# Two passes of 188 columns against two of 95, for the odd rows of every fourth wave number, in a fused Fourier mixing and ELU kernel

## The chip, the cores and the metric

The kernel runs on one core of one Trainium2 chip. The metric is the device time of one execution in microseconds (us), lower is better. Everything is computed in float32.

## The reference

```python
def _attn_ref(x):                       # x: (8, 3008, 256)
    X = np.fft.fft(x, axis=1)
    X = np.fft.fft(X, axis=2)
    return X.real.astype(np.float32)

def _moe_ref(x, w_in, w_out):           # x: the result above as (24064, 256)
    h = x @ w_in                        # w_in: (256, 2048)
    g = np.where(h > 0.0, h, 1.0 * (np.exp(np.minimum(h, 0.0)) - 1.0))
    return (g @ w_out).astype(np.float32)   # w_out: (2048, 256)
```

The real part of a two-dimensional Fourier transform is taken of each of the 8 batches (3008 rows, 256 channels), and every row of it goes through two matrix products with an ELU between them. The rows of the transform are mirror images of each other up to a sign, so the kernel computes only 1504 wave numbers k of each batch and gets the other half of the rows by a change of sign in the first product.

## The kernel before, in words

**The main loop.** The 8 times 1504 wave numbers stand as columns in two rings in SBUF, `Rr` (cosine part) and `Ir` (sine part). They are cut into 47 tiles of 256 columns. For each tile there are 8 steps, each with 256 of the 2048 hidden channels, so there are 376 steps. One step s does the following:

- TensorE: two matmuls `H<-Rr,Wsc` (`mm_P`) into a fresh PSUM bank H (there are three), later two `H<-Ir,Wsc` on top of them (`mm_Q`).
- VectorE: between these two, two instructions that read H (`even_part`, line 1339, written E), then `h_minus` (line 1353), and one step later the two ELU instructions `g_plus` and `g_minus` (line 1369), which finish the tile G of this step. The one that reads G and H is `g_plus`; with it H becomes free.
- ScalarE: four activations (two Relu, two Exp).
- GpSimd: four additions and subtractions `G<-G` of 256 columns (`sum_1`, `sum_3`, `sum_2`, `sum_4`, in that order; the second product is done by a scheme of seven products instead of eight).
- TensorE, two steps later: the seven products of the second layer into the banks pA to pD. The third of them, `pB<-G,WT`, reads the result of `sum_2`.

After every 8 steps a tile's sums are combined and transposed on VectorE (`u`, `v`, `ot`) and stored.

**The order.** Every piece of work is an event with a time on a made-up clock: step s begins at s*T, with T = 4.8, and an event stands at s*T + dt. All events are sorted by these times and issued in this order; `pin` keeps the order of each engine. So the times set only the order in each engine's queue, and an engine runs its queue strictly in this order. In step s, E stands at 0.9, `mm_Q` at 2.17, `g_plus` and `g_minus` of step s-1 at 2.2 and 2.9, `h_minus` at 3.55, and work besides goes to 4.2 or 4.25 (after `h_minus`, ahead of the next E) or to 1.0 (after E, ahead of `g_plus`).

**The transform of batches 2 to 7** (`Quarter`) is spread over the 48 steps of the main loop that come before its columns are needed. Steps of this part are counted from r0 = 48*b - 70 (for batch b = 2, r0 is 26). The 3008 rows have been folded to residues s = 0 to 752, on 94 to 96 partitions: four tiles `e`, `o` of 768 columns (near and far rows) for each part, ri = 0 (cosine) or 1 (sine), and for even or odd k (`kodd`). Each (ri, kodd) has two halves, each into one bank H: the even rows (`par` = 0) and the odd rows (`par` = 1). Each half is four passes, that is matmuls whose moving operand are columns of a constant table `QM` and whose stationary operand is one 128-column slot of the folded data. Each float32 matmul of the program is two records in the trace, each with its own weight load (PEld).

For even k the odd rows stand in two sets of 94 rows, s1 = 8p+3 or 8p+1 (slot 1 and its partner) and s3 = s1 + 376. `quarter_pairs` (GpSimd, at 46 to 49) makes sums u and differences v of each row with its mirror row, three slots in one instruction of 384 columns (line 601, `pairs<-e,o` and `o<-e,o`). The half then has these passes, with (u, v) exchanged for ri = 1:

```python
c = 378 if self.kodd else 379
for k, o in ((u, 0), (v, 189)) if self.kodd else ((u, 0),):
    yield (k, "+"), c, 95, slice(o, o + 189, 2)
    yield (k, "-"), c + 95, 94, slice(o + 1, o + 188, 2)
    c += 189
if not self.kodd:
    yield (v, 1), c, 188, slice(189, 377)
    yield (v, 3), c + 188, 188, slice(189, 377)
```

The first two passes (95 and 94 columns) give the 189 wave numbers k = 0, 4, 8 and so on; they use u1+u3 and u1-u3, which `shift_pairs` makes on VectorE. The last two (188 columns each) give the 188 wave numbers k = 2, 6, 10 and so on: one multiplies v1, the other v3, and both add into the same 188 columns.

For each of the two halves ri, `at_quarter` issues: even rows at step+0 (4.75), their reading on ScalarE (`copy`, 0.9) and VectorE (`unfold`, 1.0) at step+1, odd rows at step+2 (4.75), and at step+3 the `join` at 1.01: `plus` and `minus` add and subtract the even rows' result `es` (SBUF) and the odd rows' result (`odd`, in bank H) into the ring. With even k these are four VectorE instructions of 187 to 189 columns (`Rr<-bs,H`, `Ir<-bs,H`, line 598; more where the ring wraps), and for ri = 0 one more of one column. Step is r0+51 for ri = 0 and r0+56 for ri = 1, so the joins stand at r0+54 and r0+59. With odd k the same half already goes by passes of 95 and 94 columns in both parts, with `copy_odd` and `unfold_odd` (`spread`) ahead of its later join.

`turn` (line 870) is a VectorE instruction on 94x128: one slot times a scalar per row (from `twist_tab`), plus another slot.

Of the kernel before, what the change touches and what calls it, by code (L numbers as in the profile page):

```python
# [25 lines left out]
NE = 377  # L26
# [2 lines left out]
BE = 4 * NH  # L29
BW = BE + 3 * NE  # L30
NA = (95, 94)
QW = (944, 756)
NP = 47
SHIFT = 8 * NP
GW = 7 * TW
# [48 lines left out]
def _quarter_consts():  # L84

    p = np.arange(96)[:, None]

    def rows(m):
        s = 8 * p + m if m < 4 else 8 * (93 - p) + m
        return s, (p < (95 if m == 0 else 94)).astype(np.float64)  # L90

    low = _odd_rows()[:, None]
    valid = (p < 2 * NP).astype(np.float64)
    out = []
    for ri in range(2):
        fn = np.cos if ri == 0 else np.sin
        for kodd in range(2):

            def block(m, k):
                s, w = (low + SHIFT * (m == 3), valid) if m % 2 else rows(m)  # L100
                w = np.where(s == 0, 0.5, w)
                w = np.where(s == RUN, 0.5 if ri == kodd else 0.0, w)
                return w * fn(2.0 * np.pi * ((s * k[None, :]) % SEQ) / SEQ)

            def twist(m, n):
                s, w = (low, valid) if m % 2 else rows(m)
                a = np.arange(n)[None, :]
                phi = np.pi * s / HALF
                turn = 2.0 * np.pi * ((2 * a * s) % HALF) / HALF
                c, d = np.cos(phi), np.sin(phi)  # L110
                if ri:
                    return w * d * np.cos(turn), w * c * np.sin(turn)
                return w * c * np.cos(turn), -w * d * np.sin(turn)

            n = 94 if kodd else 95
            near = 2 * np.arange(n) + kodd
            a, b = block(0, near), block(4, near)
            if kodd:
                u1, v1 = twist(1, 189)
                u2, v2 = twist(2, 95)  # L120
                parts = [a, u2, b, v2, u1[:, ::2], -u1[:, 1::2], v1[:, ::2], -v1[:, 1::2]]
            else:
                ev, od = 4 * np.arange(189), 4 * np.arange(188) + 2
                parts = [a, b, block(2, ev[:95]), block(2, od[:94])]
                parts += [block(1, ev[::2]), block(1, ev[1::2]), block(1, od), block(3, od)]
            out += parts
    return np.concatenate(out, axis=1).astype(np.float32)


def _turn_consts():  # L130
    low = _odd_rows()
    out = []
    for s in (low, low + SHIFT, 8 * np.arange(96) + 2):
        t = np.tan(np.pi * np.minimum(s, RUN - 1) / HALF)
        out += [t, -1.0 / t, 1.0 / t, -t]
    for fn in (np.cos, np.sin):
        near, far = (fn(np.pi * s / HALF) for s in (low, low + SHIFT))
        out.append(far / near)
    return np.stack(out, axis=1).astype(np.float32)


# [34 lines left out]
def kernel(  # L176
# [386 lines left out]
            out=t[0:96, 0 : QW[kodd]], in_=QM_dr.ap()[:, n : n + QW[kodd]]  # L563
        )

    twist_tab = cpool.tile([128, 14], FP, tag="turns")

    warm = cpool.tile([128, 1], FP, tag="warm")
    nc.vector.memset(warm, 0.0)
# [30 lines left out]
    def gtt(o, a, b, op):  # L600
        pin(nc.gpsimd.tensor_tensor(out=o, in0=a, in1=b, op=op))  # L601
# [236 lines left out]
    def quarter_pairs(b, ri, kodd, m):  # L838

        near, far = state["F", ri, kodd]  # L840
        slot = lambda m: (near, far)[m // 4][0:94, 128 * (m % 4) : 128 * (m % 4) + 128]
        parts = state.setdefault(("Q", ri, kodd, b), {0: near[0:95, 0:128], 4: slot(4)})
        if not kodd:
            if m == 1:
                state["pairs"] = spool.tile(
                    [128, 384], FP, tag="side", bufs=2, name="pairs"
                )
            new = state["pairs"]
            a, z = (
                t[0:94, 128:512].rearrange("p (m d) -> p m d", d=128)  # L850
                for t in (near, far)
            )
            o = new[0:94].rearrange("p (m d) -> p m d", d=128)
            if m == 1:
                gtt(o, a, z[:, ::-1], ALU.add)
            else:
                gtt(z[:, ::-1], a, z[:, ::-1], ALU.subtract)
            for k in (1, 2, 3):
                parts["u", k] = new[0:94, 128 * k - 128 : 128 * k]
                parts["v", k] = slot(8 - k)  # L860
            return
        new = (near, near, far)[m - 1][0:94, (512, 640, 512)[m - 1] :]
        parts["u", m], parts["v", m] = new[:, 0:128], slot(1 if m == 1 else 8 - m)
        for i, o in ((0, parts["u", m]), (1, parts["v", m])):
            turn(o, slot(8 - m), 4 * (0, 2, 1)[m - 1] + 2 * ri + i, slot(m), ALU.add)

    def turn(o, a, c, b, op):

# [83 lines left out]
    class Dft:  # L952
# [27 lines left out]
        def unfold_odd(self):  # L980
            pass
# [39 lines left out]
    class Quarter(Dft):  # L1021
        def parts(self, par):

            u, v = ("v", "u") if self.ri and not self.kodd else ("u", "v")
            if not par:
                order = (
                    ((0, 94), (("u", 2), 95), (4, 94), (("v", 2), 95))
                    if self.kodd
                    else ((0, 95), (4, 95), ((u, 2), 95), ((v, 2), 94))
                )  # L1030
                c = o = 0
                for key, n in order:
                    yield key, c, n, slice(o, o + n)
                    c, o = c + n, o + n
                return
# [3 lines that stand above are left out]
                yield (k, "-"), c + 95, 94, slice(o + 1, o + 188, 2)  # L1039
                c += 189  # L1040
            if not self.kodd:
                yield (v, 1), c, 188, slice(189, 377)
                yield (v, 3), c + 188, 188, slice(189, 377)

        def mms(self, par, ps):
            parts = list(self.parts(par))
# [61 lines left out]

        def copy_odd(self):

            if self.kodd:
                self.far = spool.tile([128, NH], FP, tag="anti", bufs=2, name="far")
                act(self.far[0 : self.M, 0:189], self.odd[0 : self.M, 189:378])

        def unfold_odd(self):
            if self.kodd:
                t = spool.tile([128, NE], FP, tag="bs", bufs=BS, name="od")
                self.spread(t, self.odd, self.far, 188)
                self.odd = t

        def put(self, up, at, n, step, e, o):
            M = self.M
# [7 lines left out]
        def join(self, up):  # L1130

            M, kodd = self.M, self.kodd

            def run(t, start, step):
                return lambda i, z: t[0:M, steps_of(start + i * step, z - i, step)]

            base, top = kodd * RUN, kodd * RUN + RUN - 1
            if kodd:
                self.put(
                    up, base if up else top, NO, 1 if up else -1,  # L1140
                    run(self.es, 0, 1), run(self.odd, 0, 1),
                )
# [12 lines left out]
        def plus(self):  # L1155
# [822 lines left out]
    def at_quarter(step, b, ri, kodd, finish, join):  # L1978
        box = []

        def d():
            if not box:
                box.append(Quarter(ri, b, kodd, state["Q", ri, kodd, b]))
            return box[0]

        def half(par):
            d().ps = bank("H")
            d().mms(par, d().ps)

# [12 lines left out]

    for b in range(2, NB):
# [105 lines left out]
```

## Time and profile before

| | us |
|---|---|
| Median of 4 runs | 1910.21 (1909.8 to 1914.21) |
| The profiled execution, its time | 1909.85 |
| Its span on the core | 1908.1 |
| TensorE matmul busy | 1899.0 (100% of the span) |
| TensorE weight load busy | 1652.0 (87%) |
| VectorE busy | 1466.9 (77%) |
| GpSimd busy | 1349.6 (71%) |
| ScalarE busy | 877.1 (46%) |
| Mean granted TensorE clock | 1.0 of full speed |

The page of the profile gives each engine's busy time, the chain of work that ended last, and the costliest groups of instructions. A group's line reads: line of the kernel, engine, operation, output <- inputs, shapes, count, then busy us and mean ns of one, then the idle time of the engine just before them and what ended it. In a timeline each line has the start in us from the span's start, the time that the merged instructions cover, the engine, line, operation, tiles, shapes and count; in brackets is idle time before it and what ended that. A matmul's record is longer than the step to the next one, since matmuls are pipelined: what a matmul costs the engine is the distance of starts. VectorE's records also overlap by some 0.08 us when nothing waits.

### The profile page before, as it was taken

What the parts mean: (1) busy time and instruction counts of PE and PEld (TensorE: products, weight loads), DVE (VectorE), ACT (ScalarE), POOL (GpSimd) and SP (SyncE); (2) the same over time, 40 slices, a digit from 0 to 9 for tenths busy, and PEclk for the clock granted to TensorE, in tenths of its full rate; (3) what the DMA queues carried; (4) which work ended last, traced back from release to release, by engine and by line L of the source; (5) the groups of instructions that cost most, each with busy time, mean ns of one, the idle gap of its engine ahead of it and who ended that gap; (6) DMA issues with size and microseconds to landing.
All of it is one profiled execution on the core that took longest, in us unless ns stands there. A gap on an engine that the chain in (4) does not pass through costs nothing.

```text
span 1908.1 us, 27911 instructions
## 1 busy us (share of the span) xinstructions
PE 1899.0 (100%) x8972; PEld 1652.0 (87%) x8972; DVE 1466.9 (77%) x2788; ACT 877.1 (46%) x1711; POOL 1349.6 (71%) x1834
## 2 busy tenths in 40 slices
PE   9999999999999999999999999999999999999999
PEld 6888888888888888888888888888888888888887
DVE  8766667887878878778777787877878778777666
ACT  5754444444444444444444444444444444444443
POOL 4887657786677766777667777687766777556664
PEclk9999999999999999999999999999999999999999
DMA  9145211211011110111102111022110210100101
GB/s 339 45 33 43 57 24 46 52 24 36 12 44 41 32 33 12 46 41 30 31 19 49 34 28 30 13 56 44 24 24 16 55 21 15 17 12 15 20 12 23
DMA packets 278934, 73.80 MB, mean 39 GB/s; under 512 B 254402, under 2 KB 268998, under 8 KB 278788
## 3 DMA queue, kind: packets, MB, share of 16 engines
q1 hardware_dynamic: 270148, 61.58, 16.0%
q0 software_dynamic: 6464, 10.18, 1.7%
q8 instruction: 71, 1.16, 0.3%
q14 instruction: 75, 0.61, 0.1%
q10 hardware_dynamic: 2176, 0.26, 0.1%
HBM read 47.10 MB, written 24.80 MB: 38 GB/s over the span
## 4 chain that ended last, share of the span: by engine, by line
PE 96%; DVE 2%; DMA 1%; ACT 1%; issue 0%; POOL 0%; ACTq 0%; POOLq 0%; DVEq 0%
PE H L592 37%; PE pB L592 17%; PE pC L592 17%; PE pD L592 17%; PE pA L592 9%; DMA xl<-in_x_dram,ix 0%; DVE e L689 0%; DVE E L1339 0%; DVE o L689 0%; DVE pow L460 0%; POOL w L601 0%; ACT Wsc L604 0%; ACT G L604 0%; ACT M L604 0%; DMA wex<-wx 0%
## 5 line engine op out<-in xcount | busy, mean ns | idle before, releaser
L601 POOL TENSOR_TENSOR G<-G 128x256 f32<-128x256 f32 x1437 | 1045.9, 737 | 504.3 <-DVE G L1369 347.0
L604 ACT ACTIVATE G<-H 128x512 f32<-128x512 f32 x376 | 224.5, 597 | 929.7 <-DVE G L1353 926.0
L1339 DVE SCALAR_TENSOR_TENSOR E<-Rb,wex,H 128x256 f32<-128x256 f32 x752 | 327.8, 477 | 334.5 <-PE H L592 327.5
L592 PE MATMUL H<-Rr,Wsc 128*128 128x256 f32 x1504 | 387.9, 381 | 0.5 <-ACT Wsc L604 0.5
L592 PE MATMUL H<-Ir,Wsc 128*128 128x256 f32 x1504 | 386.9, 380 | 1.5 <-DVE E L1339 1.4
L592 PE MATMUL pC<-G,WT 128*128 128x256 f32 x1440 | 369.7, 379 | 0.0
L592 PEld LDWEIGHTS H<-Ir,Wsc 128*128 128x128 f32 x1504 | 278.6, 189 | 49.1 <-DVE E L1339 3.9
L592 PEld LDWEIGHTS H<-Rr,Wsc 128*128 128x128 f32 x1504 | 282.6, 190 | 41.1 <-issue 2.3
L592 PEld LDWEIGHTS pC<-G,WT 128*128 128x128 f32 x1440 | 274.1, 190 | 36.7
L1353 DVE SCALAR_TENSOR_TENSOR G<-E,H 128x512 f32<-128x512 f32 x376 | 257.4, 685 | 44.8 <-POOL G L601 11.4
L1369 DVE SCALAR_TENSOR_TENSOR G<-G,H 128x512 f32<-128x512 f32 x376 | 256.4, 682 | 39.6 <-ACT G L604 39.5
L1369 DVE SCALAR_TENSOR_TENSOR G<-M,G 128x512 f32<-128x512 f32 x376 | 257.4, 685 | 0.8 <-ACT M L604 0.8
L604 ACT ACTIVATE G<-G 128x512 f32<-128x512 f32 x376 | 233.4, 621 | 0.0
L592 PE MATMUL pA<-G,w 128*128 128x256 f32 x784 | 229.6, 380 | 0.0
L592 PE MATMUL pB<-G,w 128*128 128x256 f32 x784 | 229.6, 380 | 0.0
L592 PE MATMUL pD<-G,w 128*128 128x256 f32 x784 | 229.4, 379 | 0.0
L604 ACT ACTIVATE M<-G 128x512 f32<-128x512 f32 x376 | 224.2, 596 | 2.8 <-DVE G L1353 2.8
L604 ACT ACTIVATE M<-M 128x512 f32<-128x512 f32 x376 | 221.1, 588 | 0.1
L592 PE MATMUL pB<-G,WT 128*128 128x256 f32 x720 | 214.5, 380 | 0.0
L592 PE MATMUL pD<-G,WT 128*128 128x256 f32 x720 | 214.3, 379 | 0.0
L592 PEld LDWEIGHTS pA<-G,w 128*128 128x128 f32 x784 | 149.1, 190 | 20.5 <-DVE G L1369 0.3
L592 PEld LDWEIGHTS pB<-G,w 128*128 128x128 f32 x784 | 149.1, 190 | 20.2 <-PE H L592 0.2
(172 smaller groups left out, 1556.1 us busy)
## 6 DMA issues: line engine op xcount, KB each, us to landing
out_dram<-ot SPq DMA_DIRECT2D x496, 32.0 KB
xq<-in_x_dram SPq DMA_DIRECT2D x48, 94.0 KB
out_dram<-ot SPq DMA_DIRECT2D x256, 2.0 KB
Rb<-r SPq DMA_DIRECT2D x10, 376.0 KB
raw<-in_moe_w_in_dram SPq DMA_DIRECT2D x7, 512.0 KB
MC<-dft_mats SPq DMA_DIRECT2D x3, 943.5 KB
xq<-in_x_dram SPq DMA_DIRECT2D x12, 192.0 KB
xq<-in_x_dram SPq DMA_DIRECT2D x36, 64.0 KB
```

What stands on the lines that cost most here:

```text
L592: nc.tensor.matmul(out_, lhsT=lhsT, rhs=rhs, start=start, stop=stop, skip_group_check=True)
L601: pin(nc.gpsimd.tensor_tensor(out=o, in0=a, in1=b, op=op))
L604: pin(nc.scalar.activation(out=o, in_=i, func=func, **kw))
L1339: nc.vector.scalar_tensor_tensor(out=S.E[:, c], in0=Rb[:, cols(i)], scalar=wex[:, f : f + 1], in1=S.H[:, c], op0=ALU.mult, op1=ALU.add,)
L1353: nc.vector.scalar_tensor_tensor(out=two(S.G[:, 0:512])[:, :, ::-1], in0=two(S.E), scalar=2.0, in1=two(S.H), op0=ALU.mult, op1=ALU.subtract,)
L1369: nc.vector.scalar_tensor_tensor(out=o, in0=e, scalar=-1.0, in1=h, op0=ALU.add, op1=ALU.max)
```

## The change

For k = 4n+2 the angle of row s is (2n+1)*phi with phi = pi*s/752, and the row s3 = s1 + 376 turns it by an odd number of quarter circles. So the two rows' contributions can be drawn together ahead of the matmul: for each a = 0 to 94, two sums

- y-part: sum over the rows of cos(phi)*cos(4*a*phi) * y, with y = v1 - tan(phi)*v3
- z-part: sum over the rows of -sin(phi)*sin(4*a*phi) * z, with z = v1 + v3/tan(phi)

give n = 2a by their sum and n = 2a-1 by their difference (for ri = 1 with sine and cosine exchanged in the table). The change does so for even k in batches 2 to 7:

- the two passes of 188 columns become two of 95, into columns 189 to 283 and 284 to 378 of the bank H;
- y and z are made by two new `turn` instructions on VectorE for each ri (`turn_pairs`), y into free columns of the far tile, z in place of v3; they are issued at r0+51 (4.2) and r0+52 (4.25) for ri = 0, at r0+53 (4.2) and r0+57 (4.25) for ri = 1;
- in the join's step, ahead of it, a `copy_odd` on ScalarE (95 columns from H to `far`) and an `unfold_odd` on VectorE (two instructions of 94 columns, `spread`, into a new SBUF tile `od` of the pool `bs`);
- the second and fourth instruction of the join read `od` (SBUF) in place of H;
- `quarter_pairs` writes its sums for even k into free columns of the near and far tiles and not into a tile `pairs` of its own, so the one GpSimd instruction of 384 columns becomes one of 256 and one of 128;
- the constant table `QM` has 758 columns for even k, 944 before, and `twist_tab` 16 columns, 14 before.

```diff
-QW = (944, 756)
+QW = (758, 756)
...
-                parts += [block(1, ev[::2]), block(1, ev[1::2]), block(1, od), block(3, od)]
+                parts += [block(1, ev[::2]), block(1, ev[1::2]), *twist(1, 95, RUN)]
...
+    t = np.tan(np.pi * low / RUN)
+    out += [-t, 1.0 / t]
...
-            o = new[0:94].rearrange("p (m d) -> p m d", d=128)
+            z = z[:, ::-1]
+            homes = (near[0:94, 512:768], 0, 2), (far[0:94, 512:640], 2, 3)
             if m == 1:
-                gtt(o, a, z[:, ::-1], ALU.add)
+                for o, lo, hi in homes:
+                    o = o.rearrange("p (m d) -> p m d", d=128)
+                    gtt(o, a[:, lo:hi], z[:, lo:hi], ALU.add)
...
+    def turn_pairs(b, ri, k):
+
+        parts = state["Q", ri, 0, b]
+        f = "vu"[ri]
+        a, z = parts[f, 1], parts[f, 3]
+        o = z if k == "z" else state["F", ri, 0][1][0:94, 640:768]
+        turn(o, z, 14 + "yz".index(k), a, ALU.add)
+        parts[f, k] = o
...
             if not self.kodd:
-                yield (v, 1), c, 188, slice(189, 377)
-                yield (v, 3), c + 188, 188, slice(189, 377)
+                for n, k in enumerate("zy" if self.ri else "yz"):
+                    o = 95 * n
+                    yield (v, k), c + o, 95, slice(189 + o, 284 + o)
...
         def copy_odd(self):
 
-            if self.kodd:
-                self.far = spool.tile([128, NH], FP, tag="anti", bufs=2, name="far")
-                act(self.far[0 : self.M, 0:189], self.odd[0 : self.M, 189:378])
-
-        def unfold_odd(self):
-            if self.kodd:
-                t = spool.tile([128, NE], FP, tag="bs", bufs=BS, name="od")
+            c, n = (189, 189) if self.kodd else (284, 95)
+            self.far = spool.tile([128, NH], FP, tag="anti", bufs=2, name="far")
+            act(self.far[0 : self.M, 0:n], self.odd[0 : self.M, c : c + n])
+
+        def unfold_odd(self):
+            t = self.od = spool.tile([128, NE], FP, tag="bs", bufs=BS, name="od")
+            if self.kodd:
                 self.spread(t, self.odd, self.far, 188)
-                self.odd = t
+            else:
+                self.spread(t, self.odd[:, 189:284], self.far, 94)
...
-                    run(self.odd, 189 * h + first // 2, 1),
+                    run((self.odd, self.od)[h], first // 2, 1),
...
         if kodd:
             at(finish * T + 4.26, lambda: d().finish())
-            at((step + 3) * T + 0.9, lambda: d().copy_odd())
-            at((step + 3) * T + 1.0, lambda: d().unfold_odd())
+        at((step + 3) * T + 0.9, lambda: d().copy_odd())
+        at((step + 3) * T + 1.0, lambda: d().unfold_odd())
...
+        for step, dt, ri, k in (
+            (51, 4.2, 0, "y"), (52, 4.25, 0, "z"), (53, 4.2, 1, "y"), (57, 4.25, 1, "z"),
+
+        ):
+            rel(step, dt, turn_pairs, b, ri, k)
```

The order of the instructions on TensorE stays as it was, with as many of them.

More of the change, by code (lines that the diff above doesn't have):

```diff
@@ L103, in block, with twist @@
                 return w * fn(2.0 * np.pi * ((s * k[None, :]) % SEQ) / SEQ)
-            def twist(m, n):
+            def twist(m, n, span=HALF):
                 s, w = (low, valid) if m % 2 else rows(m)
                 a = np.arange(n)[None, :]
-                phi = np.pi * s / HALF
-                turn = 2.0 * np.pi * ((2 * a * s) % HALF) / HALF
+                phi = np.pi * s / span
+                turn = 2.0 * np.pi * ((2 * a * s) % span) / span
                 c, d = np.cos(phi), np.sin(phi)
@@ L564, in load_quarter_mats @@
         )
-    twist_tab = cpool.tile([128, 14], FP, tag="turns")
+    twist_tab = cpool.tile([128, 16], FP, tag="turns")
     warm = cpool.tile([128, 1], FP, tag="warm")
@@ L843, in quarter_pairs @@
         if not kodd:
[L844 to L848, printed above, removed]
             a, z = (
@@ L852, in quarter_pairs @@
             )
-            o = new[0:94].rearrange("p (m d) -> p m d", d=128)
+            z = z[:, ::-1]
+            homes = (near[0:94, 512:768], 0, 2), (far[0:94, 512:640], 2, 3)
             if m == 1:
-                gtt(o, a, z[:, ::-1], ALU.add)
-            else:
-                gtt(z[:, ::-1], a, z[:, ::-1], ALU.subtract)
+                for o, lo, hi in homes:
+                    o = o.rearrange("p (m d) -> p m d", d=128)
+                    gtt(o, a[:, lo:hi], z[:, lo:hi], ALU.add)
+            else:
+                gtt(z, a, z, ALU.subtract)
+            for o, lo, hi in homes:
+                for k in range(lo, hi):
+                    parts["u", k + 1] = o[:, 128 * (k - lo) :][:, 0:128]
             for k in (1, 2, 3):
-                parts["u", k] = new[0:94, 128 * k - 128 : 128 * k]
                 parts["v", k] = slot(8 - k)
@@ L1140, in join @@
                     up, base if up else top, NO, 1 if up else -1,
-                    run(self.es, 0, 1), run(self.odd, 0, 1),
+                    run(self.es, 0, 1), run(self.od, 0, 1),
                 )
```

## Prediction

> **What bounds the kernel now.** I read the page first: busy times, then the chain that ended last.
>
> ```profile
> PE 1899.0 (100%) x8972; PEld 1652.0 (87%) x8972; DVE 1466.9 (77%) x2788; ACT 877.1 (46%) x1711; POOL 1349.6 (71%) x1834
> ...
> PE 96%; DVE 2%; DMA 1%; ACT 1%; issue 0%; POOL 0%; ACTq 0%; POOLq 0%; DVEq 0%
> ```
>
> TensorE is busy all the time and 96% of the chain. A busy matmul engine can still wait, so the second view is the waits of TensorE over the whole run:
>
> ```profile
> PE H L592 <- DVE E L1339: 1.4, 3, 0.7
> PE H L592 <- ACT Wsc L604: 1.2, 2, 0.6
> ```
>
> These are the longest entries, and nearly all of it lies before 216 us. So in the part that the change touches (432 to 1650 us) the time is the sum of TensorE's steps: a step taken out shortens the run by its length, and whatever makes TensorE wait lengthens it by the wait. The third view is the timeline of TensorE at one odd half (batch 2, ri = 0), then at an even half, which has eight records of 94 and 95 columns:
>
> ```profile
> 442.59 0.58 PE L592 MATMUL H<-QM,e 94*128 94x95 f32 x4
> 443.01 0.83 PE L592 MATMUL H<-QM,o 94*128 94x188 f32 x4
> 443.68 1.03 PE L592 MATMUL H<-Rr,Wsc 128*128 128x256 f32 x4
> ```
>
> ```profile
> 457.06 0.36 PE L592 MATMUL H<-QM,e 95*128 95x95 f32 x2
> 457.26 0.61 PE L592 MATMUL H<-QM,o 94*128 94x95 f32 x4
> 457.70 0.39 PE L592 MATMUL H<-QM,pairs 94*128 94x94 f32 x2
> 457.93 0.84 PE L592 MATMUL H<-Rr,Wsc 128*128 128x256 f32 x3
> ```
>
> From start to next start, the odd half takes 443.68 - 442.59 = 1.085 us (to the ns) and the even half 457.93 - 457.06 = 0.865.
>
> **TensorE: what goes.** The odd half becomes eight records of 94 and 95 columns, like the even half, in the same order. The saving is 1.085 - 0.865 = 0.22 us a half. All twelve odd halves of even k (6 batches, 2 ri) measure 1.084 to 1.086, and every half of 95-column passes 0.863 to 0.866, so 12 x 0.2205 = **2.65 us**. Halving the columns doesn't halve the step: 188 columns step by 159 ns (the first of four by 190), 95 by 111 to 113, with a weight load of 190 ns per record beside each. A step as short as 84 to 86 ns stands in the trace too, once per half, in its first record.
>
> The Trainium skill, "TensorE: Matmul & The Clock Gate", section "Back-to-back issue gap", gives about 81 ns per matmul for a stream of weight loads and matmuls at 128 columns, less than the 111 ns that these rows show; by it the four records would come to 0.12 us less a half, 1.5 us in all, and the run to an estimated 1906.1. The rows are this kernel's own float32 passes of the same width, and I go by them.
>
> **VectorE: what is added.** In all 24 turns, 24 spreads of 94 columns, and 24 join instructions that read SBUF instead of H. The only question is what is queued behind them and when TensorE needs it. Here is VectorE's timeline around the first join:
>
> ```profile
> 438.91 0.87 DVE L1339 SCALAR_TENSOR_TENSOR E<-Rb,wex,H 128x256 f32<-128x256 f32 x2 [0.98 <-PE H L592]
> ...
> 441.12 0.69 DVE L1353 SCALAR_TENSOR_TENSOR G<-E,H 128x512 f32<-128x512 f32 x1
> 441.73 1.16 DVE L870 SCALAR_TENSOR_TENSOR o<-o,twist_tab,e 94x128 f32<-94x128 f32 x2
> 444.75 0.87 DVE L1339 SCALAR_TENSOR_TENSOR E<-Rb,wex,H 128x256 f32<-128x256 f32 x2 [1.85 <-PE H L592]
> 445.54 1.13 DVE L598 TENSOR_TENSOR Rr<-bs,H 128x189 f32<-128x189 f32 x4
> 446.57 0.15 DVE L598 TENSOR_TENSOR R<-bs,H 128x1 f32<-128x1 f32 x1
> 446.64 0.68 DVE L1369 SCALAR_TENSOR_TENSOR G<-G,H 128x512 f32<-128x512 f32 x1
> ```
>
> *The turns.* One takes 354 to 372 ns here when it begins with GpSimd free or just starting, 770 to 777 beside it (the pair at 441.73 is one of each). All four go ahead of an E that waits for TensorE anyway: the idle time before that E is 1.65 us at r0+52, 0.98 at r0+53, 1.85 at r0+54 and 1.21 at r0+58. Even at 0.78 each turn fits (the tightest is z, 0.78 in 0.98). I cost the four at nothing. If the cover were gone, each us past it would be a us on TensorE, since `H<-Ir` starts only 0.22 us after E's end.
>
> *The join, ri = 0.* The two spreads go between E and the join. Instructions of 94 and 95 columns step by 0.165 us (four of them fill 435.40 to 436.06 in the same timeline), so `g_plus` at 446.64 comes 2 x 0.165 = 0.33 us later against TensorE. Behind it wait `g_minus`, `h_minus` and, on other engines, these two:
>
> ```profile
> 443.51 0.72 POOL L601 TENSOR_TENSOR xq<-xq,xq 96x255 f32<-96x255 f32 x1
> 447.47 3.03 POOL L601 TENSOR_TENSOR G<-G 128x256 f32<-128x256 f32 x4 [3.23 <-DVE G L1369]
> ```
>
> ```profile
> 449.72 0.59 PE L592 MATMUL pB<-G,w 128*128 128x256 f32 x2
> 450.16 0.59 PE L592 MATMUL pB<-G,WT 128*128 128x256 f32 x2
> ```
>
> GpSimd's four sums of G start when `g_plus` is done; the third ends at 449.69 and feeds `pB<-G,WT` at 450.16, so 0.47 us lie between. Not all of that is free: where this product really waited (at 214.84), it started 0.09 after the sum's end and its next step was 0.07 longer, so 0.16 are needed and the **slack is 0.31 us**. It is 0.46 to 0.47 at four of the six joins; at 915.7 and 1151.2 (batches 4 and 5) the ring wraps, the join has two instructions more, and 0.335 - 0.16 = 0.18 is left. The stall is then 4 x (0.33 - 0.31) + 2 x (0.33 - 0.18) = **0.4 us**. Everything here moves with TensorE's 0.22 us, because E waits for TensorE in front of the join.
>
> *The SBUF operand.* For `Rr<-bs,od` of 188 columns this trace has no row; its bounds are near ones. From below: 128 columns from SBUF alone take 275 ns, as 124 from H do (277), so no difference. From above: `bs<-xq` of 188 columns, SBUF alone beside a busy GpSimd, reaches 882 to 885 against 346 from H, +0.54 each. I take nothing, since GpSimd is idle from 444.24 to 447.47 (3.23 us in the fence) and the join ends at 446.73.
>
> *The other slacks behind `h_minus`.* The E after it waits 0.98 us; ScalarE's chain has 0.38 us before `p<-pA` (449.93), which waits for TensorE. 0.33 fits in both.
>
> *The join, ri = 1.* The same 0.33 us, but an even half of TensorE lies behind, and the sum ends 1.43 us before its product (1.31 where the ring wraps): nothing.
>
> **ScalarE and GpSimd.** `copy_odd` (0.25 us, as `near<-H` of 95 columns) goes ahead of two Exp and waits for the odd half's end; the Exps end at 443.96 and `g_plus` comes at 446.64, so 2.7 us cover it; past that it would delay `g_plus` like the spreads. GpSimd's 384 columns (0.995 us) become 256 and 128 (0.73 and 0.48), 0.22 us more at r0+46 and r0+48, where it then idles 0.78 and 0.51 us: nothing; without that idle time the sums would be late, with 0.66 us or more to their product. The smaller table is six batches' constant, loaded once each: nothing.
>
> The Trainium skill, "GPSIMD Engine Reference", section "Key points", says that GpSimd shares its SBUF interfaces with VectorE and contends with instructions of two SBUF inputs, as all the added turns and SBUF joins are. The rows bear that out (354 against 777), and by the rule alone the join would pay the +0.54 twice, which is the second rival below.
>
> **Sum.** -2.65 + 0.4 = -2.25 us on the profiled execution's 1909.85 gives 1907.6. Three of the four runs and the profile lie at 1909.8 to 1910.21; the median shown is 0.36 above the profile, and I put half of that on top: **1907.8**.
>
> **The rivals.**
> - *The join's spreads cost more.* If the new dependences (spread on `far`, join on `od`) each lose the 0.08 us overlap of records, g_plus is 0.49 late: 4 x 0.18 + 2 x 0.31 = 1.3 us. Result 1909.85 - 2.65 + 1.3 + 0.2 = 1908.7. Against it: an instruction stands between the second spread and its reader.
> - *Slower: the SBUF joins meet GpSimd.* At the six joins of ri = 0, `g_plus` is then 0.33 + 2 x 0.54 = 1.41 us late, and `pB<-G,WT` stalls 4 x 1.10 + 2 x 1.23 = 6.9 us; 1909.85 - 2.65 + 6.9 + 0.2 = 1914.3. It decides from a lateness of about 0.7 us on (6 x 0.44 eats 2.65). For it: `Rr<-bs,od` of 376 columns takes up to 1073 ns at the joins of odd k. Against it: GpSimd's idle time around this join, in all six batches.
> - *The saving is hidden* (TensorE waits for something right after, in every half, or the short passes take what the long ones did): 1909.9 to 1910.2. Against it: no wait of TensorE over 0.2 us between 216 and 1890 us.
> - *Passes are shorter than the 111 ns*: at the 86 ns of the first records, 48 x 0.0255 = 1.2 us more; with no stall 1909.85 - 2.65 - 1.2 + 0.2 = 1906.2. Against it: from the second record on, none of the short passes goes below 109.
>
> **How the numbers follow.** About 0.2% (3.8 us) is what a measurement of this kernel can tell from no change. Chances: forecast (1907.2 to 1908.3) 0.66; costlier spreads 0.09; hidden 0.08; shorter passes 0.09 (faster by over 0.2%, below 1906.4); meeting GpSimd 0.08, of which 0.07 above 1914.0. So faster 0.09, same 0.84, slower 0.07. The range leaves out the last two cases: 1906.7 to 1910.0; the upper end takes in the hidden case, the lower a forecast without stall and shorter by 0.5 us.
>
> **What would show it.** Right: odd halves of 0.865 us; E at r0+54 still waiting for TensorE; `g_plus` 0.33 us later after E; gaps of `pB<-G,WT` under 0.2 us, in batches 4 and 5 above all. Wrong: an `Rr<-bs,od` far over 0.35 us, an E without idle time ahead of it at r0+52 to r0+58, a new wait of TensorE on VectorE or GpSimd in its list of waits.

## The result, and the profile after

The changed kernel takes **1907.34 us** (median of 32 runs, 1906.59 to 1911.62), the kernel before 1909.79 us (median of 52 runs, 1909.02 to 1919.6). The ratio is 0.9987 with a 95% interval of 0.9982 to 0.9992. So it is faster, by 2.45 us between the medians, and inside the 0.2% that the prediction counts as no change. The profiled execution took 1906.76 us, with a span of 1904.9 at a granted clock of 1.0.

First the page after: busy times, then the chain that ended last.

```profile
PE 1897.0 (100%) x8972; PEld 1649.5 (87%) x8972; DVE 1487.9 (78%) x2836; ACT 879.4 (46%) x1723; POOL 1350.8 (71%) x1846
...
PE 96%; DVE 2%; ACT 1%; DMA 0%; issue 0%; POOL 0%; ACTq 0%; SPq 0%; DVEq 0%; POOLq 0%
```

The balance is the same. TensorE has as many records as before (8972) and 2.0 us less busy time. VectorE has 48 instructions more (24 turns, 24 spreads) and 21 us more busy time, in a run that is shorter. That work was hidden, so what is left to explain is on TensorE.

Next, the timeline of TensorE at the first odd half after the change (start, length, engine, line, operation, operands, records).

```profile
441.34 0.58 PE L594 MATMUL H<-QM,e 94*128 94x95 f32 x4
441.76 0.61 PE L594 MATMUL H<-QM,o 94*128 94x95 f32 x4
442.21 1.06 PE L594 MATMUL H<-Rr,Wsc 128*128 128x256 f32 x4
443.10 0.59 PE L594 MATMUL pA<-G,w 128*128 128x256 f32 x2
```

From the first record of the half to the first of `H<-Rr` it is 0.87 us instead of 1.085, as forecast. But look one group further: `H<-Rr` takes 0.89 us to `pA` (442.21 to 443.10). Behind the long passes the same four records took 0.86. Record by record, in ns from start to start (the last four steps are those of `H<-Rr`):

```
before  86 110 111 111 | 190 160 159 159 | 220 215 215 215
after   86 110 110 112 | 113 111 112 112 | 245 216 217 215
```

Of the 220 ns that the short passes save, the first step behind them takes back 25.

To place the rest, I cut both runs at the first and last record of a scalar product (`QM`) on TensorE. The part ahead starts with the kernel, the section between holds everything that the change touches, and the part behind is output.

| | first `QM` record at | section | from the last `QM` record to the end |
|---|---|---|---|
| before | 432.20 us | 1256.45 us | 219.43 us |
| after | 430.95 us | 1254.53 us | 219.43 us |

The section is 1.92 us shorter. Step by step its records give:

- twelve odd halves, 0.2205 us shorter each: -2.65 us
- the step behind each of them, 0.0255 us longer: +0.31 us
- a stall of `pB<-G,WT` at the join in batches 4 and 5: 0.155 and 0.160, together +0.32 us
- the same place in the four other batches, 0.017 to 0.024 each: +0.08 us
- all else: +0.02 us

Of the 1.25 us by which the section starts earlier, 0.86 has built up by 17 us into the run and all by 114 us, long before anything that the change computes. What it is belongs to the last experiments.

### The profile page after: what moved, and what is told of

It is laid out like the page before. It is cut to its first block, busy times and chain, and to the rows that moved or that the text cites. A ratio compares the mean times of both kernels' runs of the same rounds, so it can differ in the third digit from the quotient of the medians.

```text
span 1904.9 us, 27983 instructions
## 1 busy us (share of the span) xinstructions
PE 1897.0 (100%) x8972; PEld 1649.5 (87%) x8972; DVE 1487.9 (78%) x2836; ACT 879.4 (46%) x1723; POOL 1350.8 (71%) x1846
## 4 chain that ended last, share of the span: by engine, by line
PE 96%; DVE 2%; ACT 1%; DMA 0%; issue 0%; POOL 0%; ACTq 0%; SPq 0%; DVEq 0%; POOLq 0%
PE H L594 37%; PE pB L594 17%; PE pC L594 17%; PE pD L594 17%; PE pA L594 9%; DVE e L691 0%; DVE o L691 0%; DVE pow L462 0%; DVE E L1352 0%; POOL w L603 0%; DMA xl<-in_x_dram 0%; ACT Wsc L606 0%; ACT G L606 0%; ACT M L606 0%; DVE w L420 0%
```

## The experiments

**Theories.** *A (the prediction's):* the time is the sum of TensorE's steps. The short passes take out 12 x 0.22 us, and the spreads return about 0.4, because they delay `g_plus`, GpSimd's sums of G and so `pB<-G,WT`. *B:* the missing part went elsewhere, into the short passes themselves or into some other effect of the added work. *C:* GpSimd and VectorE meet at the SBUF operands, so that the join costs far more. The first two experiments part A from B by making one half of the change alone.

### The added work alone

Edit of the kernel before: turns, copies and spreads are made, into columns and tiles that nothing reads; passes and join stay.

```diff
+        turn(state["F", ri, 0][1][0:94, 512 + n : 640 + n], z, 14 + "yz".index(k), a, ALU.add)
...
+            t = self.od = spool.tile([128, NE], FP, tag="bs", bufs=BS, name="od")
             if self.kodd:
...
+            else:
+                self.spread(t, self.odd[:, 189:284], self.far, 94)
```

> The kernel before with all that the change adds and nothing that it removes: the four turns of each batch (y and z into spare columns), copy_odd and the two spreads, but the passes of 188 columns stay and the join reads H as before; the new tile od is not used. Theory (everything added lies beside TensorE, but for the join of ri = 0 where the ring wraps): TensorE's odd halves stay at 1.085 us, the product that reads the third sum stalls 0.15 us in batches 4 and 5 and by under 0.03 in the others, so +0.3 to +0.4 us on the kernel before, ratio 1.0002. Rival (the added VectorE work costs something at each of the twelve halves): 12 x 0.165 us or more, so +2 us or more, ratio 1.001 and up, with TensorE's waits on VectorE in the list.

Measured: 1909.8 us against 1909.58 of the kernel before, ratio 0.9999 (0.9991 to 1.0008). In the trace the section is 1256.76 us, 0.31 longer than before. `g_plus` starts 2.22 us after E (2.35 where the ring wraps) instead of 1.89, and the stall is almost all at the two wraps. So 24 turns and 24 spreads (20 us of VectorE) and 12 more copies on ScalarE cost TensorE 0.3 us in six batches. B's second form (some other effect of the added work) is out.

### The short passes alone

Edit of the changed kernel: no turns and no spreads; the passes take rows 1 and 3 as they are, and the join reads H. It leaves out the combination of those rows, so wave numbers 2, 6, 10 and so on are not the reference's.

```diff
-                for n, k in enumerate("zy" if self.ri else "yz"):
+                for n, k in enumerate((1, 3)):
...
-                    run((self.odd, self.od)[h], first // 2, 1),
+                    run(self.odd, 189 * h + first // 2, 1),
...
-            rel(step, dt, turn_pairs, b, ri, k)
+            pass
```

> The changed kernel with the two short passes alone: no turns, no copy_odd, no spreads for even k, and the join reads H; what it leaves out is the combination of the rows 1 and 3, so the wave numbers 2, 6, 10 and so on of batches 2 to 7 are not the reference's. Theory: the odd halves take 0.865 us and nothing stalls at the joins, so -2.65 us on the kernel before (ratio 0.9986) and 0.3 us less than the changed kernel. Rival (the saving is larger on TensorE and partly lost to the added work): more than 3.2 us under the kernel before.

Measured: 1906.79 against 1909.58 us, ratio 0.9985 (0.9976 to 0.9994). In the trace the section is 1254.14 us, 2.30 shorter than before, without a stall. The passes alone are worth 2.30 us, not 2.65. The steps of its first odd half are 86, 110, 111, 111, 113, 111, 112, 112 and then 246, so the 26 ns behind each half belong to the short passes: 12 x 0.0255 = 0.31. B's first form holds for that part. The kernel before has them behind each of its even halves too; at the first one `H<-Rr` takes 0.89 us to `pA`:

```profile
433.07 1.06 PE L592 MATMUL H<-Rr,Wsc 128*128 128x256 f32 x4
433.96 0.60 PE L592 MATMUL pA<-G,w 128*128 128x256 f32 x2
```

In its odd halves about as much stands in the first long pass (190 ns against 159 or 160 of the others), inside the 1.085 us. So the two halves that the prediction compares were not cut at like places.

### The stall taken away

The wait of batches 4 and 5 is easy to miss. The list of TensorE's waits has no entry for it. It shows in TensorE's timeline of the changed kernel, as a step that is too long, and, below it, in the row of the weight loads:

```profile
918.12 0.60 PE L594 MATMUL pA<-G,w 128*128 128x256 f32 x2
918.55 0.60 PE L594 MATMUL pB<-G,w 128*128 128x256 f32 x2
919.03 0.70 PE L594 MATMUL pB<-G,WT 128*128 128x256 f32 x2
```

```profile
918.33 0.41 PEld L594 LDWEIGHTS pB<-G,w 128*128 128x128 f32 x2
919.03 0.30 PEld L594 LDWEIGHTS pB<-G,WT 128*128 128x128 f32 x2 [0.29 <-POOL G L603]
```

The first `pB` starts 0.43 after `pA`, the second 0.48 after the first, and its pair of records lasts 0.70 instead of 0.60: 0.05 and 0.10 are lost. The weight load names the releaser, GpSimd's sum of G. In this edit `g_minus` and `h_minus` stay in their place, and the half of the join that nothing needs so soon goes behind them:

```diff
-        at(t + 0.001, lambda: d().minus())
+        at(t + (0.001 if kodd or ri else 3.25), lambda: d().minus())
```

> The changed kernel with one event moved: for ri = 0 of even k the minus half of the join is issued at 4.25 of the same step (behind h_minus) and not at 1.0 (ahead of g_plus). Theory: g_plus comes 0.6 us earlier, the two stalls of 0.15 us in batches 4 and 5 are gone, the idle time before the next E is used up to the same degree, so -0.3 us on the changed kernel, seen in the trace rather than in the time. Rival (the idle time before the next E is needed for something else): a new wait of TensorE on E in the step after, 0.1 us or more at each of six joins, and the time is the changed kernel's or above.

Measured: 1906.99 against 1909.58 us, ratio 0.9988 (0.9979 to 0.9996). In the trace `g_plus` starts 1.64 us after E (1.77 in batch 4), the sum ends 0.58 to 0.73 us ahead of its product, and the section is 1254.14 us, 0.38 shorter than with the whole change. TensorE's timeline of this kernel at the same place:

```profile
918.30 0.59 PE L594 MATMUL pA<-G,w 128*128 128x256 f32 x2
918.73 0.59 PE L594 MATMUL pB<-G,w 128*128 128x256 f32 x2
919.16 0.59 PE L594 MATMUL pB<-G,WT 128*128 128x256 f32 x2
```

Every group starts 0.43 behind the one before it. So the stall is 0.4 us in all and comes from the join's length, as A has it. This version has the lowest median of those that compute everything; against the changed kernel the 0.35 us (0.14 when each is set against the kernel before that was measured beside it) are too little for a timed difference, and only the traces tell them apart.

### What a short pass costs

If the passes are limited by their columns, halving them again saves; if by the weight load that each record brings, it costs. The first edit cuts each pass of 95 into 48 and 47. The second, made when the first was measured, pads the table with zeros and makes the passes 128 columns wide, 33 of them of no use.

```diff
-                    o = 95 * n
-                    yield (v, k), c + o, 95, slice(189 + o, 284 + o)
+                    for o, m in ((95 * n, 48), (95 * n + 48, 47)):
+                        yield (v, k), c + o, m, slice(189 + o, 189 + o + m)
```

> The changed kernel with each of the two passes of 95 columns cut into one of 48 and one of 47 with the same stationary operand, so the same columns in twice as many records. Theory (a record cannot step faster than its weight load, 111 ns, however few its columns): four records more of 111 ns a half, and the shorter ones are no faster, so 12 x 0.446 = +5.3 us on the changed kernel. Rival (the step goes with the columns): +0 to +1 us, since the columns are the same in all.

```diff
-                    o = 95 * n
-                    yield (v, k), c + o, 95, slice(189 + o, 284 + o)
+                    o = 128 * n
+                    yield (v, k), c + o, 128, slice(189 + o, 317 + o)
```

> The changed kernel with 33 columns of zeros behind each of the two passes of 95, so that they have 128 columns (the result is the same, since the added columns are not read). Theory (a short record steps by its weight load, 111.4 ns, until its columns take longer; 256 columns step by 216 ns, so 128 take 108): no change, within 0.1 us from the first to the last pass of the quarter transforms. Rival (the step goes with the columns): 4 x 12 x 33 x 0.84 ns = +1.3 us.

Measured: split, 1912.54 against 1909.58 us, ratio 1.0013 (1.0004 to 1.0023), section 1259.92 us, 5.39 longer than with the change; wide, 1907.21 against 1909.92 us, ratio 0.999 (0.9981 to 0.9999), section 1254.51 us, 0.01 shorter. TensorE's timeline of the split kernel, then of the wide one:

```profile
441.92 1.02 PE L594 MATMUL H<-QM,o 94*128 94x48 f32 x8
442.76 1.11 PE L594 MATMUL H<-Rr,Wsc 128*128 128x256 f32 x4
443.70 0.59 PE L594 MATMUL pA<-G,w 128*128 128x256 f32 x2
```

```profile
442.23 0.64 PE L594 MATMUL H<-QM,o 94*128 94x128 f32 x4
442.71 1.03 PE L594 MATMUL H<-Rr,Wsc 128*128 128x256 f32 x4
443.57 0.59 PE L594 MATMUL pA<-G,w 128*128 128x256 f32 x2
```

Eight records of 48 and 47 columns take 0.84 us to the next group, four of 95 took 0.45, four of 128 take 0.48. Behind them `H<-Rr` takes 0.94, 0.89 and 0.86. In ns:

```
95 columns   86 110 110 112 | 113 111 112 112                | 245
48 and 47    86 110 110 112 | 73 112 98 111 126 112 97 112   | 299
128 columns  86 110 111 112 | 140 111 112 112                | 220
```

Half and excess behind it belong together. With that step at its usual 220 ns, the three are 866 + 25 = 891, 1259 + 79 = 1338 and 894 + 0 = 894 ns, which is 8, 12 and 8 times 111.4 (891, 1337, 891) to 3 ns. A short record costs 111.4 ns whether it has 47, 95 or 128 columns, and what it doesn't show in its own step it leaves to the next. In the split kernel 4 x 111.4 ns x 12 halves = 5.35 us, against 5.39 measured.

What keeps this pace is the weight load that each record brings. TensorE's weight loads in the split kernel:

```profile
441.83 0.97 PEld L594 LDWEIGHTS H<-QM,o 94*128 94x128 f32 x8
442.73 0.52 PEld L594 LDWEIGHTS H<-Rr,Wsc 128*128 128x128 f32 x3
```

The eight loads take 0.90 us to the next group, and from the second load of the half to the second of `H<-Rr` each starts 111 to 113 ns behind the one before it, while the records themselves step by anything from 73 to 126. The changed kernel's loads step by 111 to 113 there too. So the second record of `H<-Rr` comes late because its load does. No experiment changes the number of columns that a load has, so how the 111.4 ns depend on it is not shown.

The Trainium skill, "TensorE: Matmul & The Clock Gate", section "LDWEIGHTS (loading the stationary operand)", puts a load at the columns of the weights over 1.2, in ns: an estimate of 107 for 128 columns. The 111.4 measured here is near that, and the 81 ns of the section that the prediction weighed is not reached.

### The price of a late join

Is the stall the lateness of `g_plus` minus a fixed slack? Two or six more spreads (into columns that nothing reads) stand behind the real ones at the joins of ri = 0:

```diff
+                if not self.ri:
+                    for _ in range(2):
+                        vtt(t[0 : self.M, 188:282], self.odd[0 : self.M, 189:283], self.far[0 : self.M, 0:94], ALU.add)
```

> The changed kernel with two more VectorE instructions of 94 columns (from H, into columns of od that nobody reads) behind the spreads of ri = 0, ahead of the join: g_plus comes 2 x 0.165 = 0.33 us later at six joins. Theory (the join's slack is used up: 0.02 us of stall at four joins and 0.155 at the two where the ring wraps, in the trace of the changed kernel): every further us of lateness is a us of TensorE, so 6 x 0.33 = +2.0 us on the changed kernel. Rival (the slack is larger and the two stalls have another cause): less than +1 us.

> As the run with two more instructions of 94 columns, with six: 0.99 us later at six joins. Theory: 6 x 0.99 = +5.9 us on the changed kernel, slower than the kernel before by some 3.5 us; the stall is seen at the product that reads the third sum, 1.0 us at each join. Rival (another wait takes part of it, since E of the next step has idle time ahead of it): under +4 us, or, if the next E becomes late as well, over +7 us.

Measured: two more, 1910.3 against 1909.49 us, ratio 1.0003 (0.9993 to 1.0012), section 2.98 longer than with the change; six more, 1917.6 against 1909.49 us, ratio 1.0047 (1.0032 to 1.0062), section 9.85 longer. Both are above A's number, and VectorE's timeline of the kernel with six more shows why:

```profile
445.15 2.02 DVE L600 TENSOR_TENSOR od<-H,far 128x94 f32<-128x94 f32 x8
447.09 0.34 DVE L600 TENSOR_TENSOR Rr<-bs,H 128x189 f32<-128x189 f32 x1
```

The two real spreads step by 0.165 us, but the eight take 1.94 up to the join. The added ones all write the same columns, and each that follows such a write steps by 0.28 to 0.29 us. The miss was in my edit: `g_plus` was 0.454 and 1.62 us later than with the change, not 0.33 and 0.99. With the measured lateness the law holds. Compared step by step with the changed kernel, TensorE loses 0.444 to 0.453 us at each of the six joins with two more, and 1.62 with six more: the lateness itself, to 10 ns. TensorE's timeline with six more:

```profile
448.43 1.10 PE L594 MATMUL H<-Rr,Wsc 128*128 128x256 f32 x4 [0.23 <-DVE R L600]
...
450.07 0.59 PE L594 MATMUL pB<-G,w 128*128 128x256 f32 x2
451.30 0.70 PE L594 MATMUL pB<-G,WT 128*128 128x256 f32 x2 [0.63 <-POOL G L603]
```

Here the wait is long enough to get a name on TensorE itself, and a second one has joined it: `H<-Rr` waits for the join's last instruction, since bank H isn't free. That stall (0.39 us in its step and 0.35 in the three behind it) is paid first, and `pB<-G,WT` pays the rest (0.88), so the sum is still 1.62.

To separate the edit's fault from the law, two added spreads went into columns of their own:

```diff
+                    for n in range(2):
+                        o = 188 + 94 * n
+                        vtt(t[0 : self.M, o : o + 94], self.odd[0 : self.M, 189:283], self.far[0 : self.M, 0:94], ALU.add)
```

> The run with two more instructions of 94 columns again, with the two writing different columns of od. In the run before they wrote the same columns and g_plus came 0.454 us later, not 0.33. Theory (an instruction that writes where the one before it writes waits for its end; without that it steps by 0.165): g_plus 0.33 us later than in the changed kernel. From the traces so far the stall is the lateness against the kernel before, less 0.31 us (0.18 where the ring wraps), so 4 x 0.35 + 2 x 0.48 = 2.4 us in place of 0.4, +2.0 us on the changed kernel from the first to the last pass of the quarter transforms. Rival (each such instruction costs 0.22 us or more whatever it writes): +2.9 us as before.

Measured: 1909.42 against 1909.92 us, ratio 0.9999 (0.9989 to 1.0008); the section is 2.26 longer than with the change. The added spreads step by 0.163 us, `g_plus` comes 0.66 us later than in the kernel before, and the six joins stall 0.32 to 0.34 us each more than with the change, 1.98 in all, against 2.0 by the law. A's law stands, with a slope of one above the slack. The other 0.3 us are three waits of 0.07 to 0.14 at 884, 894 and 1500 us, far from these joins. They also come in the first kernel with two more, and not in the one with six (which has two others, of 0.04 and 0.09). Each is `H<-Ir` behind an E of VectorE that comes late; why it comes late there stays open.

### GpSimd beside the join

The prediction's rival on the slower side said that SBUF operands next to a busy GpSimd cost 0.54 us each. GpSimd idles there, so this edit gives it two sums to do at the join of even k (ri = 0), into columns that nothing reads:

```diff
+        gtt(e[0:94, 512:700], t[0:94, 0:188], t[0:94, 0:188], ALU.add)
...
+            for n in range(2):
+                at((step + 3) * T + 1.001 + 0.001 * n, lambda: busy(d().od))
```

> The changed kernel with two GpSimd additions of 188 columns at each join of ri = 0 (od plus od, into columns that nobody reads any more), which can start when the spreads are done and so run beside the two SBUF joins. Theory (an instruction with two SBUF inputs waits for a GpSimd instruction beside it; rows of the kernel before: 128x188 from SBUF 0.60 to 0.88 us beside a busy GpSimd, 0.35 in the changed kernel with GpSimd idle): g_plus 0.5 to 1.07 us later at six joins, so +3.0 to +6.4 us on the changed kernel, slower than the kernel before at the upper end. Rival (the added GpSimd work costs nothing here): Rr<-bs,od stays at 0.35 us and the time within 0.4 us of the changed kernel's.

Measured: 1910.0 against 1909.49 us, ratio 1.0003 (0.9994 to 1.0013); section 2.78 longer than with the change. VectorE and GpSimd in this kernel:

```profile
445.60 0.34 DVE L600 TENSOR_TENSOR Rr<-bs,H 128x189 f32<-128x189 f32 x1
445.86 0.68 DVE L600 TENSOR_TENSOR Rr<-bs,od 128x188 f32<-128x188 f32 x1
446.46 0.34 DVE L600 TENSOR_TENSOR Rr<-bs,H 128x187 f32<-128x187 f32 x1
446.72 0.39 DVE L600 TENSOR_TENSOR Rr<-bs,od 128x188 f32<-128x188 f32 x1
```

```profile
445.83 1.07 POOL L603 TENSOR_TENSOR e<-od 94x188 f32<-94x188 f32 x2 [2.35 <-DVE od L600]
```

The read of `od` that starts with GpSimd's first sum takes 0.68 us, the next one, near the end of the two sums, only 0.39, and the rows from H stay at 0.34 in both places. The total is a little under the expected range, as one of the two reads paid in full and the other hardly; in batch 5 more was lost, 0.89 us against 0.32 to 0.39 at the other joins.

The trace shows the rule behind these sizes. All ten reads of 188 columns that start while a GpSimd instruction runs end 0.211 to 0.214 us after the end of that instruction, whether they take 0.39 or 0.68. In the trace of before, the 24 of `bs<-xq` (0.60 to 0.885 us) end 0.208 to 0.213 us after it. So the read waits for the end of the GpSimd instruction that was there first, and pays much or little by how much of it is left. It works the other way as well: GpSimd's next instruction, where it starts behind the read, takes 0.83 us, and 0.72 else. In batch 5 the ring wraps, the second read is two instructions, and GpSimd's next one gets in between them; the two reads then take 0.97 us. GpSimd behind the second read in batch 2, then VectorE and GpSimd in batch 5:

```profile
446.86 0.83 POOL L603 TENSOR_TENSOR xq<-xq,xq 96x255 f32<-96x255 f32 x1
```

```profile
1153.39 0.97 DVE L600 TENSOR_TENSOR Rr<-bs,od 128x40 f32<-128x40 f32 x2
```

```profile
1153.47 0.72 POOL L603 TENSOR_TENSOR xq<-xq,xq 96x255 f32<-96x255 f32 x1
```

And the changed kernel, VectorE at the same place, with GpSimd idle:

```profile
443.30 0.87 DVE L1352 SCALAR_TENSOR_TENSOR E<-Rb,wex,H 128x256 f32<-128x256 f32 x2 [0.86 <-PE H L594]
444.09 0.41 DVE L600 TENSOR_TENSOR od<-H,far 128x94 f32<-128x94 f32 x2
444.42 0.35 DVE L600 TENSOR_TENSOR Rr<-bs,H 128x189 f32<-128x189 f32 x1
444.68 0.35 DVE L600 TENSOR_TENSOR Rr<-bs,od 128x188 f32<-128x188 f32 x1
444.94 0.34 DVE L600 TENSOR_TENSOR Rr<-bs,H 128x187 f32<-128x187 f32 x1
445.20 0.35 DVE L600 TENSOR_TENSOR Rr<-bs,od 128x188 f32<-128x188 f32 x1
...
445.53 0.68 DVE L1382 SCALAR_TENSOR_TENSOR G<-G,H 128x512 f32<-128x512 f32 x1
```

From SBUF or from H, the row is 0.35 or 0.34 long. Theory C has the right mechanism, and it doesn't act here because of GpSimd's idle time.

### The part ahead of the section

The changed kernel reached its first scalar product 1.25 us earlier. One candidate of the program's own is the smaller table. Here it gets its old width in DRAM back, with zeros; the load into SBUF stays at 758 columns:

```diff
+                parts += [np.zeros((96, 186))]
...
-        n = sum(QW[i % 2] for i in range(2 * ri + kodd))
+        n = sum((944, 756)[i % 2] for i in range(2 * ri + kodd))
```

> The changed kernel, with 186 columns of zeros in the constant table for each even-k part, so that the table in DRAM is as wide as before; the loads take the same 758 columns and no other instruction changes. In the traces the first pass of a quarter transform starts at 432.2 us in the kernel before, 433.1 with the additions alone, and 430.95 to 431.2 in the three kernels with the narrow table. Theory A (that is the chance of each execution's first loads): time and section as the changed kernel's, the start anywhere from 430.9 to 433. Theory B (the table's size moves something in the first 430 us): about +0.5 us on the changed kernel, with the start at 432 or later.

Measured: 1907.49 against 1909.49 us, ratio 0.9992 (0.9983 to 1.0001); first `QM` record at 431.57 us, section 0.05 longer than with the change. So one trace speaks against the width in DRAM. The load of the table is no better a candidate: it is issued at 214 us before and at 217 us after the change, when the early start is already there. Then both kernels were profiled once more, unchanged:

> The kernel before, unchanged, profiled a second time, for one question: is the 1.25 us by which the changed kernel reached its first scalar product earlier (430.95 against 432.20 us) chance of the execution or the program's own? Theory, chance: the start falls anywhere from 430.9 to 432.2 and the section behind it is again 1256.45 within 0.05. Rival, the program: it starts again at 432.0 or later. This decides only whether some 0.5 us of the difference of the medians belong to the change.

> The changed kernel, unchanged, profiled a second time, for the same question. Theory, chance: the first scalar product starts anywhere from 430.9 to 432.2, and the section behind it is again 1254.5 within 0.05. Rival, the program: it starts at 430.9 to 431.5 as in most kernels with the short passes.

Measured: before, 1909.55 us, first `QM` record at 431.9 us, section 1256.45 us again; after, 1907.43 us, first record at 431.56, section 1254.58. The section repeats to 0.06 us. The start moves by 0.3 us in the one kernel and by 0.6 in the other, and the gap between the two shrank from 1.25 to 0.34. So most of the early start was chance of the execution. Whether a few tenths of it belong to the program stays open. The medians hint that they do: against the kernel before, nine of the ten kernels with the short passes are 0.1 to 0.8 us faster than their section accounts for (one is 0.2 slower), and the one with the additions alone 0.1. Each of these differences lies within its own interval.

## Why the prediction was right, and where it was not

The forecast was 1907.8 us, the median is 1907.34, and "within 0.2%" had the chance of 0.84. Step by step:

- **TensorE is the bound, and the time is the sum of its steps:** right. In every experiment the halves, the step behind them and the joins account for the section to 0.05 us, but for the waits far from the joins in the three kernels with more spreads (0.3, 0.1 and 0.3 us), while VectorE gained 21 us unseen.
- **An odd half becomes 0.865 us:** right, 0.864 to 0.867. **12 x 0.2205 = 2.65 us is the saving:** this term was mis-sized. The saving is 2.3 us (short passes alone, 2.30), because I measured the half up to the start of `H<-Rr` and stopped there. The next step is 246 ns behind short passes and 220 behind long ones. The trace of before showed it: the even half that I took as the pattern has the 246 ns behind it too, and the odd half has the same excess inside, in its step of 190. Comparing two halves needs both ends at records that both kernels have alike, and `H<-Rr` started alike but did not step alike.
- **The join is 2 x 0.165 = 0.33 us later:** right, 0.334. **Slack 0.31, or 0.18 at a wrap; stalls 4 x 0.02 + 2 x 0.15 = 0.4 us:** right in place and size, 0.017 to 0.024 at four joins and 0.155 to 0.160 at the two wraps, and 0.38 us came back when the stall was taken away.
- **The SBUF operand at nothing:** right, 0.35 against 0.34 us, and for the reason given, GpSimd's idle time.
- **The turns at nothing:** right. The added ones take 0.35 to 0.76 us, but at r0+52 and r0+54 the turn behind the added one now takes 0.88 next to GpSimd, where it took 0.35 to 0.37 before. The idle time ahead of the E at r0+54 shrinks from 1.85 us to 1.06 with the additions alone, and to the 0.86 in the last timeline above; the least, 0.47, is left at r0+53. None of it reaches TensorE. **The join of ri = 1, the copies, GpSimd's split:** right, no stall there.
- **The sum, -2.25 us:** the section shows -1.92, so 0.3 us too much, all of it from the mis-sized term. The median moved by 2.45, and a difference of 1.92 lies inside its interval (0.18% to 0.08%, which is 3.4 to 1.5 us). That the forecast lies as near to the median as it does is partly luck: the 0.3 us too much on the saving meets 0.5 us that the medians differ outside the section.
- **The rivals:** costlier spreads did not come (one instruction between spread and reader was enough: 0.334 us). Hidden saving and passes shorter than 111 ns did not come; the second is excluded by the split, which shows 111.4 ns as the least. Meeting GpSimd is a real mechanism, shown with GpSimd made busy, that lacks its condition here; there it made `g_plus` 0.39 us late at four joins, 0.32 and 0.90 at the two that wrap, not the 1.08 of two full prices.

## What to carry to other kernels

When a record is made shorter, count up to the first later record that starts *and steps* as before: work that an engine has queued ahead, here the weight loads, can be owed by the step behind. Below some 128 columns a float32 pass of this kernel costs its weight load, so the number of passes counts, not their width. And before work is put in front of a join, find the consumer with the least slack and look at every batch: the two that wrapped had 0.18 us where the others had 0.31, and they made most of the stall.

## What was not expected of the hardware

- A record with 128 columns of weights takes 111.4 ns at least, and is not credited with less: 47, 95 and 128 columns came to the same sum with the step behind.
- A product whose weight load waits loses more than the wait: it starts 54 ns after the sum's end, and the next step is 104 ns longer, so a sum has to end 0.158 us ahead of its product's start to cost nothing.
- Instructions of VectorE that write the columns of the one before step by 0.28 to 0.29 us, where the same instruction into other columns steps by 0.163.
- A VectorE instruction of 188 columns with both inputs from SBUF that starts while a GpSimd instruction runs ends some 0.21 us after that one's end: 0.39 us in the mildest case seen at the join, 0.68 in the other, up to 0.885 in the trace of before, against 0.35 without. With one input from H it stays at 0.34.
